# Linear attention and an RWKV channel mix: both head groups of batches 5 to 7 in one tiled block, and the last two tiles stored by one DMA a piece

## Chip, cores and metric

One core of one Trainium2 chip. The metric is the device time of one execution in microseconds (us); the median of three runs is given. A profile of one further execution shows where the time goes. PE is TensorE, DVE VectorE, ACT ScalarE, POOL GpSimd, SP SyncE.

## What is computed

q, k and v are [8 batches, 8 heads, 576, 64] in float32. Linear attention with two softmaxes gives x, which is read as [8, 576, 512] and goes through a channel mix with weights of 512 x 1024, 1024 x 512 and 512 x 512:

```python
q_s = softmax(q, axis=-1)                     # over head_dim
k_s = softmax(k, axis=2)                      # over the sequence
kv  = einsum('bhsd,bhse->bhde', k_s, v)       # 64 x 64 for each head
x   = einsum('bhsd,bhde->bhse', q_s, kv).transpose(0, 2, 1, 3).reshape(8, 576, 512)

x_prev = x shifted by one row (a zero row first)
xk = mu_k * x + (1 - mu_k) * x_prev
xr = mu_r * x + (1 - mu_r) * x_prev
k  = maximum(xk @ w_k, 0)
v  = k * k @ w_v
r  = sigmoid(xr @ w_r)
out = r * v                                   # float32, [8, 576, 512]
```

## The kernel before

**Stages.** A batch is worked in two head groups g = 0, 1 of four heads. For each group `attention(b, g)` loads q, k, v (three loads of 576 KB on POOL's queue, L213, into one of 11 "raw" buffers), takes the exponentials on ACT, sums and scales q on DVE, and casts v. On PE follow the small matrices KV = k_s' v (`kv`, L420: 36 matmuls of 64x64 tiles with 65 columns, the 65th being the sum that normalises k), on DVE the reciprocal of that sum (`rz`) and the weights (`w`), and on PE X = q_s kv (`x`, L577: eight matmuls of 64x64 tiles, four for the last 64 of the 576 columns and four for the first 512). X needs q turned; for batches 4 to 7 (`CROSS`) a DMA transpose that SP issues does that (`tq`). ACT copies X out of PSUM in two parts (`xb`, 512 columns from a pair of banks, and `xs`, the 64 spare columns), DVE shifts and mixes it into xk and xr.

The channel mix runs over units of up to 512 rows (`unit`: k matmuls L681, relu on ACT L660, square on DVE L670) and over 36 tiles of 128 rows (`tile_out`: r matmuls L714, tanh `th` on ACT L719, v matmuls L734, the gate `o` on DVE L740 that makes the output in a "th" buffer, stores `st` L750). The mix of batches 0 to 3 runs while the attention of later ones is made.

**Blocks on PE.** For batches 2 to 7 a PE block B(b, g) holds the X of the group before it ("pending") and the KV of its own group, so that X does not stand alone between full 128x128 matmuls. The spare 64 columns of X lie beside KV in one PSUM pair (columns 368 on, KV from 296), the 512 in the other pair. Only X of (2, 1) and of (7, 1), named in `ALONE`, have a block of their own. The last blocks of before are B50, B51, B60, B61, B70, B71 and X71.

**PSUM.** Four single banks mm_a to mm_d serve k, r and v; two pairs att_a and att_b serve the attention.

**Stores.** An output tile is 128 rows of a ring, two sequence positions j and j+1 of 64 rows each. `store` writes one half: 64 partitions of the buffer to 64 rows that lie 9 x 512 elements apart, as a destination of [64 rows][width]. Two such DMAs store a tile, both from SP's queue; in the last two tiles (34 and 35) the second goes by ACT's queue. Tile 35 is cut into two pieces of 256 columns, each with its own v matmuls, gate and two stores.

**The order.** What each engine does and in which order is not found at build time. `ORDER` is a list of the names of all operations in one line of time, with the buffer that each takes after the colon ("B51:1.0", "th35:1"), an engine ahead of "!" where there is a choice, and "^" for a load that is held until another operation is done ("load71q0^tq50"). `Plan.ordered` reads it and fails if an operation stands ahead of what it needs; semaphore waits follow from the data. "fill" and "fillgap" are matmuls on idle data in the start. A name with ".2" is the second operation of that name; "v35_0.2" is the first half of the v matmuls of tile 35's second piece.

Of the kernel before, what the change touches and what calls it, by code (L numbers as in the profile page):

```python
# [38 lines left out]
GAPS = 11  # L39
WHOLE = ((0, 0), (0, 1), (1, 0), (1, 1), (2, 0), (3, 0))  # L40
FUSED = (0, 1)
CROSS = (4, 5, 6, 7)
EARLY_UNITS = 3
ALONE = ((2, 1), (B - 1, 1))
# [5 lines left out]
ACT!load01k1:3 SP!load01k0 warm POOL!muload expq000:0 expq001 load00v^expq000 rsum000:0 rsum001  # L50
load01v expq010:1 wk00 expq011 rrec001 rrec000 rsum010:1 wide:0 wk01 expk000:0 rrec010 rsum011
wk10 mu:1 expk001 fillgap:2 fillgap.2:3 fillgap.3:2 fillgap.4:3 scale010:0 wk11 Z00:0 fillgap.5:2
fillgap.6:3 fillgap.7:2 fillgap.8:3 fillgap.9:2 fillgap.10:3 fillgap.11:2 rrec011 expk011:1
load11q0:4 scale011 widecopy rz00:0 scale001:1 T01:1 KV000 scale000 ACT!qt011:0 KV001 expk010
DVE!qt010 T00 rest mucopy kvn00:0 KV010 qt001:1 POOL!wp001:0 DVE!qt000 Z01 KV011 edge00 load10q0:5
wp000 X0010:3 rz01:1 load11q1 X0001:2 kvn01:1 edge01 x0010 wp010:1 load10q1 X0000:0 wp011 x0001a
X0100:1 load11v1:6 ACT!x0001b X0110:3 x0000a wr X0101:2 x0100b ACT!x0000b x0110 X0011:0 load11k1:7
DVE!x0101a x0100a k0_4:2 x0101b k1_7:3 x0011 k1_3:0 load10v1:8 k1_7.2 k1_3.2 relu1_7:0 k0_4.2
load11k0 k1_0:1 relu1_3:1 sq1_7 k0_5 expq110:2 k0_0:3 load11v0 k1_0.2 k0_0.2 relu0_4:2 rsum110:2
k1_4:0 relu1_0:0 k1_5:2 sq1_3 expq111 k1_2:1 sq0_4 k1_5.2 sq1_0 k1_2.2 rsum111 relu1_5:1 k1_4.2  # L60
cast111:0 k0_1 relu1_2:2 k0_6:2 sq1_5 wv0 relu1_4:0 k1_6:1 rrec110 expq101:1 sq1_2 k0_2:0
scale110:2 load10k1:9 k0_6.2 relu0_0:1 X0111:1 load10v0 rrec111 k0_7 expq100 rsum101:3 k1_6.2
k1_1:3 relu0_6:2 load10k0 k0_2.2 rrec101 k1_1.2 sq0_0 ACT!x0111 k0_3 rsum100 wv1 r0:2 relu1_1:1
sq0_6 expk111:2 wv2 r1:3 sq1_4 rrec100 th0:0 load20q0:10 scale100:0 relu1_6:2 r2:2 th1:1
load21q0:0 sq1_6 scale111 ACT!cast110 r3:1 sq1_1 relu0_2:0 scale101 T11:0 expk110 T10:1
ACT!cast101:1 KV11 qt101:2 load20v0:1 v3_0:3 qt110:1 sq0_2 th3:2 qt111 v0_0:0 rz11:2 expk101:0
cast100 kvn11:0 DVE!qt100 v1_0:1 edge11 expk100 wp110:0 edge10 DVE!wp111 X1100:0 KV10 x1100 v0_1
rz10:0 kvn10:1 X1111:0 POOL!wp100:1 X1101:1 x1111 v1_1 ACT!x1101 load31q0:2 X1001:0 th2:3 X1000:1
load20k0:3 ACT!x1001 v0_2 DVE!x1000 v3_1 load21v0:4 expq200:0 o0 v1_2 load21k0:5 k2_7:2 k2_3:0
rsum200:1 expq210:2 wp101 k2_7.2 v3_2 load30q0:6 relu2_7:2 o1 X1011:0 X1110:1 cast200:2 load30k0:7  # L70
rrec200 k2_3.2 o3 k2_1:2 load40q0:8 k2_0:1 relu2_3:1 x1011 k2_1.2 load30v0:9 expq310:1 sq2_3
k2_0.2 scale200:1 load41q0:10 k2_2:3 k2_6:0 relu2_1:0 load31k0:0 relu2_0:1 X1010:0 k2_2.2
expk200:1 sq2_0 k2_6.2 DVE!x1010 k2_5:2 load31v0:1 v2_0:1 relu2_2:1 sq2_1 rsum210:0 cast210:0
k2_4:3 load40k0:2 TKV20:0 relu2_6:0 sq2_2 rrec210 expk210:2 k2_4.2 rz20:1 sq2_6 k2_5.2 sq2_7
load40v0:3 v6_0:0 DVE!x1110 relu2_5:1 relu2_4:0 w20:0 v2_1 scale210:2 expq300:0 r5:2 load50q0:4
r6:3 qt20:0 rsum310:2 load50k0:5 v2_2 expk300:0 sq2_5 B21:1.0 sq2_4 o2 load41v0:6 th6:4 v6_1
rz21:2 xb20:0 w21:1 rsum300:3 r4:1 load50v0:7 xs20 qt21:1 r7:3 edge20 o6 th4:5 rrec300 X21:0.1
st6.2 diff20:0 th7:6 r8:0 th5:7 sc2001:0 scale300:0 v4_0:1 xb21:1 v5_0:3 xs21 sc2011:1 cast300:1
sc2010 v7_0:2 sc2000 edge21 rrec310 expq400:2 diff21:1 load70k0:9 TKV30:0 sc2100:2 expq410:0 v5_1
sc2101 load70v0:8 rz30:0 mix210 v4_1 cast310:2 load51v0:10 mix200 v7_1 o5 th8:8 v4_2 load51q0:1  # L80
sc2111:2 k3_1:3 st5.2 expk400:1 o4 w30:2 k3_3:0 st4 o7 relu3_1:2 load41k0:2 st0.2 expk310:2 sc2110
k3_7:1 mix201 st1 k3_0:3 sq3_1 st6 qt30:2 load51k0:0 scale310:1 st5 k3_2:2 relu3_0:1 st1.2
cast400:0 sq3_0 B31:1.0 rsum400:1 relu3_2:0 k3_6:3 load60k0:3 xs30:0 mix211 relu3_7:2 k3_5:2
relu3_3:1 rz31:1 sq3_2 xb30 w31:0 k3_4:1 sq3_3 sq3_7 relu3_6:0 r9:0 edge30 rrec400 diff30:0 qt31:0
# [12 lines left out]
sq5_2 v13_1 rz50:1 edge41 w50:0 mix400 expk600:2 r15:2 diff41:0 v15_1 expq610:0 o12 scale600:1
B51:1.0 th15:5 r14:0 expk700:0 sc4101:0 sc4100 r17:2 o15 mix410 st15.2 v17_0:3 th17:6 o13 th14:0
k6_0:2 tq51^load71k0:1 rz51:2 expq710:2 v17_1 w51:1 mix401 k6_1 o17 xs50:0 xb50 k6_4:1 sc4111:2
v16_0:0 st17 rsum610:3 expq700:1 st10 k6_6:3 st8.2 k6_5 edge50 relu6_0:0 sc4110 v16_1 st17.2  # L100
diff50:1 cast710:0 st12 k6_2:2 mix411 st13.2 relu6_4:2 B60:1.0 o16 st3.2 k6_3 xb51:1 rz60:0
sc5001:0 tq60^load71k0:2 k6_7 sc5000 sq6_0 r20:1 relu6_6:1 mix500 xs51 v14_0:0 relu6_2:0 sq6_6
w60:2 st13 sc5010:1 r18:3 sc5011 st16 edge51 th20:8 diff51:0 st9 r19:2 expk610:1 rrec610 st16.2
sc5101:2 v14_1 sc5100 st15 th19:6 sq6_2 mix510 v18_0:1 th18:2 sq6_4 cast610:1 o14 k7_7:2 sc5110:0
expk710:2 k7_0:3 scale610:0 B61:0.1 cast700:2 sc5111 tq61:0 v18_1 mix511 rsum700:0 xs60:1 k7_3:0
relu7_7:1 st12.2 relu7_0:0 st9.2 k7_4:2 relu7_3:2 xb60 r21:3 sq7_3 rz61:1 rsum710:2 k7_5:0
relu7_4:2 k7_2:2 edge60 w61:0 o18 B70:1.0 rrec700 sq7_4 mix501 v19_0:1 relu7_5:2 th21:1 diff60:1
r22:0 xs61:0 xb61 sq7_0 sq7_7 k7_1:3 scale700:2 relu7_2:0 v19_1 relu7_1:1 edge61 tq70:1 sq7_1
r26:2 rrec710 sq7_5 sq7_2 r23:3 th26:3 diff61:0 st14 v22_0:2 st10.2 th23:5 sc6110:2 rz70:2 sc6111
th22:7 k7_6:3 sc6100:0 o19 v20_0:0 scale710:1 relu7_6:1 r25:1 w70:1 tq71:2 sc6001:1 B71:0.1 sq7_6  # L110
th25:9 sc6101 v23_0:3 mix611 st14.2 sc6000 v21_0:1 mix610 rz71:0 v23_1 mix600 xs70:0 xb70 w71:2
v21_1 o23 v22_1 X71:0.1 o22 v20_1 sc6011:2 sc6010 k8_5:3 edge70 diff70:0 k8_3:2 o21 relu8_5:2
mix601 k8_0:3 relu8_3:0 sc7001:0 o20 k8_1:1 relu8_0:1 sq8_3 xb71:1 st20.2 k8_2:2 sq8_0 st18 k8_6:0
st20 relu8_2:0 relu8_1:1 st21 r28:3 st23 sq8_1 sc7000 r27:2 relu8_6:1 st18.2 mix700 xs71 th28:4
k8_4:1 edge71 sq8_5 diff71:1 r24:0 sq8_6 sq8_2 k8_7:3 th24:0 sc7100:1 sc7101 relu8_4:2 v27_0:0
sc7010:2 mix710 relu8_7:1 r29:1 sc7111:0 sq8_7 sq8_4 v24_0:3 th29:8 sc7110 th27:2 k9_4:1 k9_6:2
relu9_4:0 k9_3:1 v24_1 relu9_3:1 relu9_6:2 sq9_3 v26_0:1 o24 k9_1:2 sc7011 sq9_4 sq9_6 v25_0:3
relu9_1:1 v26_1 k9_2:2 o26 v25_1 relu9_2:0 v27_1 o25 k9_0:1 o27 mix711 k10_6:2 st27 st25 sq9_1
k9_7:3 relu10_6:2 st19 relu9_0:1 sq10_6 r30:0 st27.2 sq9_0 st26.2 mix701 k10_3:2 st24 k10_0:1
# [69 lines left out]
def graph(kn):  # L189
# [144 lines left out]
    def attention(b, g):  # L334
# [139 lines left out]
        else:  # L474
# [4 lines left out]
            def block():  # L479
                if turn_x:  # L480
                    turn_x[0](qtp)
# [144 lines left out]
    for b in range(B):  # L626
        for g in range(2):
            attention(b, g)
# [271 lines left out]
```

## Time and profile before

| | us |
|---|---|
| median of 3 runs (196.58 to 196.68) | 196.65 |
| the profiled execution | 196.49 |
| its span, first to last instruction | 194.7 |
| TensorE busy in it (95%) | 184.9 |
| DVE busy (76%) | 148.4 |
| ACT busy (69%) | 133.7 |
| POOL busy (24%) | 46.4 |

The granted TensorE clock is 0.995 of full over the span. In the rows of the timeline a line gives the start, the duration, the engine (PEld is the load of weights, SPq and ACTq the issuing of DMAs), the line of the code, the operation, output<-input, the shape and how many were grouped. The rows of waits give an engine and line, what it waited for, and the total, number and longest in us. In the windows each engine's busy time stands with the number of instructions, then the granted clock, the busy share of the 16 DMA engines and GB/s. In the DMA rows the last number is the median time from issue to landing.

### The profile page before, as it was taken

Reading aid. Unit: us, or ns where it says so; the run is one execution under the profiler, and the core shown is the slowest. Engines: PE = TensorE matmul, PEld = TensorE weight load, DVE = VectorE, ACT = ScalarE, POOL = GpSimd, SP = SyncE. Lnnn points to the kernel's source line nnn. Section 1 sums busy time; section 2 is a strip of 40 time slices with the busy share of each in tenths; the row PEclk is TensorE's granted clock in tenths of the full one; section 3 lists DMA queues with packets and bytes.
Section 4 is the critical chain, followed back from the end, with each engine's and each line's share of the span. In section 5 each row is a group of like instructions: output and inputs, shape, how many; then the busy total and the mean of one; then the engine's idle time right before and its main releaser. Section 6 shows DMA issues by size and latency. Waiting matters only on the chain.

```text
span 194.7 us, 4639 instructions
## 1 busy us (share of the span) xinstructions
PE 184.9 (95%) x1819; PEld 93.9 (48%) x1841; DVE 148.4 (76%) x343; ACT 133.7 (69%) x214; POOL 46.4 (24%) x76
## 2 busy tenths in 40 slices
PE   7897999999999999999999999999999999999990
PEld 2374755445545544465545644444444444444450
DVE  1886887689999999998998998999669247324431
ACT  3856999899999999489997988663175522621400
POOL 6857663885416303200700000000000000000000
PEclk9999999999999999999999999999999999999998
DMA  5999999999999999979997794144015003703855
GB/s 190 350 204 338 300 306 307 327 397 394 391 392 394 400 411 331 331 246 203 231 407 183 179 206 88 32 100 96 7 35 130 0 0 83 188 3 80 201 123 135
DMA packets 26069, 42.45 MB, mean 218 GB/s; under 512 B 11828, under 2 KB 15168, under 8 KB 26048
## 3 DMA queue, kind: packets, MB, share of 16 engines
q0 software_dynamic: 9504, 28.00, 43.8%
q1 hardware_dynamic: 15728, 12.72, 27.1%
q10 hardware_dynamic: 816, 1.44, 2.0%
q8 instruction: 14, 0.23, 0.5%
q14 instruction: 7, 0.06, 0.1%
HBM read 33.56 MB, written 9.44 MB: 221 GB/s over the span
## 4 chain that ended last, share of the span: by engine, by line
PE 80%; DVE 7%; DMA 6%; issue 2%; ACT 1%; POOL 1%; ACTq 0%; DVEq 0%; POOLq 0%
PE mm_c L681 10%; PE mm_b L734 9%; PE mm_a L734 8%; PE mm_d L734 8%; PE mm_b L681 8%; PE mm_d L681 7%; PE mm_c L714 5%; PE mm_c L734 4%; PE mm_a L681 4%; PE mm_d L714 4%; PE mm_a L714 3%; DMA mu_rows<-in_moe_mu_r_dram 3%; DMA raw_c<-in_q_dram 3%; PE mm_b L714 3%; DVE k L670 1%
## 5 line engine op out<-in xcount | busy, mean ns | idle before, releaser
L734 PEld LDWEIGHTS <-k 128*128 128x128 bf16 x296 | 28.1, 98 | 30.6 <-issue 0.7
L714 PEld LDWEIGHTS <-xr 128*128 128x128 bf16 x144 | 13.9, 98 | 16.4 <-issue 0.2
L670 DVE TENSOR_TENSOR k<-rel_b 128x512 bf16<-128x512 bf16 (+2 forms) x29 | 11.6, 399 | 8.9 <-ACT rel_b L660 8.8
L660 ACT ACTIVATE rel_a<-mm_c 128x512 bf16<-128x512 f32 (+1 forms) x11 | 6.6, 599 | 9.7 <-PE mm_c L681 9.6
L714 PE MATMUL mm_c<-wr,xr 128*128 128x512 bf16 x47 | 12.3, 379 | 0.1
L681 PEld LDWEIGHTS <-wk_aa 128*128 128x128 bf16 x88 | 8.4, 98 | 7.8 <-issue 0.2
L681 PEld LDWEIGHTS <-wk_ba 128*128 128x128 bf16 x88 | 8.3, 98 | 7.8 <-issue 0.4
L670 DVE TENSOR_TENSOR k<-rel_a 128x512 bf16<-128x512 bf16 (+2 forms) x24 | 9.6, 400 | 3.2 <-ACT rel_a L660 3.2
L670 DVE TENSOR_TENSOR k<-rel_c 128x512 bf16<-128x512 bf16 (+2 forms) x23 | 9.3, 403 | 3.4 <-ACT rel_c L660 3.3
L681 PEld LDWEIGHTS <-wk_ab 128*128 128x128 bf16 x88 | 8.4, 98 | 7.1 <-issue 0.5
L681 PEld LDWEIGHTS <-wk_bb 128*128 128x128 bf16 x88 | 8.5, 98 | 6.8
L734 PE MATMUL mm_b<-wv_a,k 128*128 128x512 bf16 x42 | 11.2, 379 | 0.1
L714 PE MATMUL mm_d<-wr,xr 128*128 128x512 bf16 x40 | 10.3, 379 | 0.0
L734 PE MATMUL mm_a<-wv_a,k 128*128 128x512 bf16 x38 | 10.2, 379 | 0.1
L734 PE MATMUL mm_d<-wv_a,k 128*128 128x512 bf16 (+1 forms) x38 | 9.8, 368 | 0.1
L681 PE MATMUL mm_c<-xk,wk_ba 128*128 128x512 bf16 (+3 forms) x34 | 8.6, 334 | 0.0
L681 PE MATMUL mm_c<-xk,wk_bb 128*128 128x512 bf16 (+3 forms) x34 | 8.6, 334 | 0.0
L714 PE MATMUL mm_a<-wr,xr 128*128 128x512 bf16 x31 | 8.2, 380 | 0.1
L660 ACT ACTIVATE rel_c<-mm_c 128x512 bf16<-128x512 f32 (+1 forms) x8 | 4.8, 595 | 4.5 <-PE mm_c L681 2.9
L681 PE MATMUL mm_c<-xk,wk_aa 128*128 128x512 bf16 (+2 forms) x28 | 7.4, 347 | 0.0
L681 PE MATMUL mm_c<-xk,wk_ab 128*128 128x512 bf16 (+2 forms) x26 | 7.0, 344 | 0.0
L660 ACT ACTIVATE rel_b<-mm_d 128x512 bf16<-128x512 f32 (+2 forms) x10 | 5.8, 577 | 1.5 <-PE mm_d L681 1.5
(352 smaller groups left out, 495.4 us busy)
## 6 DMA issues: line engine op xcount, KB each, us to landing
raw_k<-in_q_dram POOLq DMA_DIRECT2D x4, 576.0 KB, 8.1
raw_f<-in_k_dram POOLq DMA_DIRECT2D x3, 576.0 KB, 8.2
raw_a<-in_k_dram POOLq DMA_DIRECT2D x3, 576.0 KB, 11.5
out_dram<-th_b SPq DMA_DIRECT2D x10, 128.0 KB, 2.4
out_dram<-th_c SPq DMA_DIRECT2D x10, 128.0 KB, 2.4
raw_b<-in_v_dram POOLq DMA_DIRECT2D x2, 576.0 KB, 10.4
raw_d<-in_k_dram POOLq DMA_DIRECT2D x2, 576.0 KB, 8.8
raw_e<-in_v_dram POOLq DMA_DIRECT2D x2, 576.0 KB, 6.3
```

The costliest lines, as they stand in the source:

```text
L660: kn.nc.scalar.activation(out=kn.rels[rel.index][:, 0:width], in_=kn.bank(kf)[:, 0:width], func=ACT.Relu, scale=HALF_ROOT)
L670: kn.nc.vector.tensor_tensor(out=to, in0=src, in1=src, op=ALU.mult)
L681: kn.nc.tensor.matmul(kn.bank(kf)[:, lo:lo + n], lhsT=kn.wk[fc // 4][ct % 2][:, ct // 2, (fc % 4) * 128: (fc % 4) * 128 + 128], rhs=kn.xs[ ...
L714: kn.nc.tensor.matmul(kn.bank(rps), lhsT=kn.xs[1][:, ct, c:c + 128], rhs=kn.wr[:, ct, :], start=(ct == 0), stop=(ct == CT - 1))
L734: kn.nc.tensor.matmul(kn.bank(vps)[:, 0:width], lhsT=kn.k2[:, ft, at:at + 128], rhs=wv_of(ft)[:, part], start=(ft == 0), stop=(ft == FT - 1))
```

## The change

- **Joint blocks.** Batches 5, 6 and 7 (`JOINT`) have one block each, D5, D6, D7, in place of two. `joint_batch` puts the KV of both groups into one PSUM pair (columns 0 and 66 on) after the X of the groups that are pending, with their spare columns at 136 and 200 of the same pair. D5 holds X41 and KV50, KV51; D6 holds X50, X51, KV60, KV61; D7 likewise; XX7 holds X70 and X71. One reciprocal (`rz5`) and one weight operation (`w5`) serve both groups; the buffers `ws` and `rzs` are doubled for it. `attention` becomes a generator that stops at the block and goes on after it.
- **A pair of single banks.** The 512 columns of the X of group 1 that such a block takes (X41 too) go to a pair "pr" made of two of the single banks, mm_a and mm_b or mm_c and mm_d, and ACT copies them in two halves (`xb51a`, `xb51b`).
- **Stores.** For tiles 34 and 35 `store_both` writes a whole piece by one DMA: 128 partitions to a destination of [2][64 rows][width]. Tile 34 goes by SP, tile 35's columns 256 on by ACT and its first columns by SP.
- **Start.** 9 gap fills in place of 11, and the rows of mu lie in the last "th" buffer in place of one of their own.
- **Order.** `ORDER` is another text throughout. Among much else, the X matmuls of batch 1 stand otherwise among the v matmuls, the loads held by "^" change (six on POOL's queue from load61q0 on, behind tq41, the third of them load50v0; before, five from load71q0 on, behind tq50), and at the end v35_0 stands ahead of v35_1.2.

A set `TWO` of batches, and the code for it, is empty and has no effect.

```diff
-GAPS = 11
+GAPS = 9
+JOINT = (5,6,7)
+KVJ, XJ = 66, 136
-ALONE = ((2, 1), (B - 1, 1))
+ALONE = ((2, 1),)
+          ("pr", 0): [("mm", 0), ("mm", 1)], ("pr", 1): [("mm", 2), ("mm", 3)]}
...
-        pair = Slot("att")
+        late = b + 1 in JOINT or b == B - 1
+        pair = Slot("pr" if late and g else "att")
...
+            if pair.pool == "pr":
+                evs += [add("ACT", lambda u=u: copy_first(u), [made], [xb], [pair],
+                            name=f"xb{tag}{'ab'[u]}") for u in range(2)]
...
+    def two_turns(name, a, ready, given, kvs):
+        turns = list(pending)
+        pending.clear()
+        def block():
+            for g, turn in enumerate(turns):
+                turn[0](a, XJ + 64 * g)
+            for g, kv in enumerate(kvs):
+                kv(a, at=KVJ * g)
+        made = add("PE", block, ready + [d for t in turns for d in t[1]] + alone,
+                   [a] + [x for t in turns for x in t[2]],
+                   given + [x for t in turns for x in t[3]], name=name)
...
+    def joint_batch(b, parts):
+        a = Slot("att")
+        rz, w = parts[0][3:]
+        made = two_turns(f"D{b}", a, parts[0][1] + parts[1][1], parts[0][2] + parts[1][2],
+                         [p[0] for p in parts])
...
+    two_turns(f"XX{B - 1}", Slot("att"), [], [], [])
...
+            def store_both(queue, part=part, width=width):
+                jb = (RING * half + c) // 64
+                bb, j = jb // J, jb % J
+                dst = bass.AP(tensor=kn.out.tensor,
+                              offset=kn.out.offset + (bb * S + j) * C + part.start,
+                              ap=[[C, 2], [J * C, 64], [1, width]])
+                kn.queues[queue].dma_start(out=dst, in_=kn.ths[th.index][:, part])
...
-            for i in range(2):
-                queue = "ACT" if last and i else "SP"
-                add(queue, lambda i=i, q=queue, f=store: f(i, q), [o], [], [th],
-                    name=f"st{index}")
+            if last:
+                queue = "ACT" if len(parts) == 2 and part.start else "SP"
+                add(queue, lambda q=queue, f=store_both: f(q), [o], [], [th], name=f"st{index}")
+            else:
+                for i in range(2):
+                    add("SP", lambda i=i, f=store: f(i, "SP"), [o], [], [th], name=f"st{index}")
...
-    kn.ws = buffers("w", [128, 2, D], BF16)
+    kn.ws = buffers("w", [128, 2, 2, D], BF16)
-    kn.rzs = buffers("rz", [128, 2], F32)
+    kn.rzs = buffers("rz", [128, 2, 2], F32)
-    kn.mu_rows = const.tile([2, 2, 256], F32, name="mu_rows")
+    kn.mu_rows = kn.ths[-1][0:2, :].rearrange("p (m c) -> p m c", m=2)
```

The end of the order, before and after:

```diff
-... v35_0.2:3 st28.2 v33_0:2 o32 st32.2 v34_0:1 st32 v33_1 v34_1 o33 r35:0 st33 o34 v35_1.2
-st34.2 st34 v35_0:2 th35:1 st33.2 v35_1 o35.2 st35.4 st35.3 o35 st35.2 st35
+... v34_0:0 st28 v32_1 st31 st24.2 v35_0.2:3 o32 st28.2 v33_0:2 st32.2 r34:1 v33_1 th34:5 st32
+v34_1 o33 r35:1 st33.2 o34 st33 v35_0:2 th35:4 st34 v35_1.2 v35_1 o35.2 o35 st35.2 st35
```

More of the change, by code (lines that the diff above doesn't have):

```diff
@@ L55 @@
[L55 to L60, printed above, removed]
@@ new lines @@
+rrec000 expq010:1 rsum001 wk00 expq011 rsum010:1 wide:0 wk01 rsum011 expk001:0 wk10 rrec010 mu:1
+expk000 rrec011 fillgap:2 fillgap.2:3 fillgap.3:2 scale010:0 wk11 Z00:0 scale011 fillgap.4:2
+fillgap.5:3 fillgap.6:2 fillgap.7:3 expk011:1 load11q0:4 rrec001 T01:1 expk010 rz00:0 load11q1
+scale001:1 fillgap.8:2 fillgap.9:3 widecopy scale000 load10q1:5 KV001 qt010:0 KV000 rest ACT!qt011
+T00 Z01 kvn00:0 KV011 qt001:1 POOL!wp001:0 DVE!qt000 KV010 mucopy edge00 load10q0 wp000 X0010:3
+rz01:1 load11k1:6 X0000:0 kvn01:1 edge01 x0010 wp010:1 X0001:2 wp011 x0000a wr X0101:1 DVE!x0001a
@@ L127 @@
+sq10_7 v32_0:1 st25 th33:3 st27.2 v34_0:0 st28 v32_1 st31 st24.2 v35_0.2:3 o32 st28.2 v33_0:2
+st32.2 r34:1 v33_1 th34:5 st32 v34_1 o33 r35:1 st33.2 o34 st33 v35_0:2 th35:4 st34 v35_1.2 v35_1
+o35.2 o35 st35.2 st35
 """
@@ L339, in attention @@
             for n in ("eq", "ek", "vv", "stat", "qs", "qt", "rz"))
[L340 removed]
+        w = None if fused or (b in JOINT and g) else in_turn("w")
         c0 = S * (b % 4)
@@ L577, in x, with copy_first, copy_second @@
                         kn.nc.tensor.matmul(kn.half(slot, u)[two[r], to:to + n],
-                                            lhsT=kn.ws[w.index][two[u], r, :], rhs=by,
+                                            lhsT=kn.ws[w.index][two[u], wg, r, :],
+                                            rhs=by,
                                             start=True, stop=True)
-        def copy_first():
-            kn.nc.scalar.copy(out=kn.xbs[xb.index][:, :, 64:576], in_=kn.whole(pair))
-        def copy_second(other):
+        def copy_first(u=None):
+            to = kn.xbs[xb.index]
+            if u is None:
+                kn.nc.scalar.copy(out=to[:, :, 64:576], in_=kn.whole(pair))
+            else:
+                kn.nc.scalar.copy(out=to[:, u, 64:576], in_=kn.half(pair, u))
+        def copy_second(other, spare):
             kn.nc.scalar.copy(out=kn.xbs[xb.index][:, :, 576:640],
-                              in_=kn.whole(other)[:, :, XO:XO + 64])
+                              in_=kn.whole(other)[:, :, spare:spare + 64])
         def edge():
@@ L619, in attention, with block @@
             other = Slot("att")
-            alone.append(add("PE", lambda: x(other), [qcopy, wdone], [pair, other], [qt, w],
+            alone.append(add("PE", lambda: x(other, XO), [qcopy, wdone], [pair, other], [qt, w],
                              name=f"X{tag}"))
-            then(alone[-1], other)
+            then(alone[-1], other, XO)
         else:
             pending.append((x, [qcopy, wdone], [pair], [qt, w], then))
-    for b in range(B):
-        for g in range(2):
-            attention(b, g)
+    def two_turns(name, a, ready, given, kvs):
+        turns = list(pending)
+        pending.clear()
+        def block():
+            for g, turn in enumerate(turns):
[5 more added lines that the diff above has]
+                   given + [x for t in turns for x in t[3]], name=name)
+        for g in reversed(range(len(turns))):
+            turns[g][4](made, a, XJ + 64 * g)
+        return made
@@ new lines, in finish, with both @@
+    def finish(part, value):
+        try:
+            part.send(value)
+        except StopIteration:
+            pass
+    for b in range(B):
+        groups = [attention(b, g) for g in range(2)]
+        if b in JOINT:
+            done = joint_batch(b, [next(part) for part in groups])
+            for part in groups:
+                finish(part, done)
+        elif b in TWO:
+            parts = [next(part) for part in groups]
+            def both(parts=parts):
+                for slot, _, _, turn, kv in parts:
+                    turn(slot)
+                    kv(slot)
+            made = add("PE", both, parts[0][1] + parts[1][1] + alone, [p[0] for p in parts],
+                       parts[0][2] + parts[1][2], name=f"TT{b}")
+            for part in groups:
+                finish(part, made)
+        else:
+            for part in groups:
+                for _ in part:
+                    pass
```

222 lines of the change are left out of this document (121 added, 101 removed).

## The prediction

> **What bounds the kernel now.** I read the page's busy times first, then its chain, then the waits of TensorE, then the tail in order of time, and last the packets of the DMA queues.
>
> ```profile
> PE 184.9 (95%) x1819; PEld 93.9 (48%) x1841; DVE 148.4 (76%) x343; ACT 133.7 (69%) x214; POOL 46.4 (24%) x76
> ...
> PE 80%; DVE 7%; DMA 6%; issue 2%; ACT 1%; POOL 1%; ACTq 0%; DVEq 0%; POOLq 0%
> ```
>
> TensorE (PE) is busy for 184.9 of 194.7 us and holds 80% of the chain that ended last; DVE and ACT have a quarter of the span free. Where PE stands still is the next question. The first three rows are all its waits from 17.7 to 191 us, the next two the largest before.
>
> ```profile
> PE mm_d L734 <- issue: 0.2, 1, 0.2
> PE mm_b L734 <- issue: 0.2, 1, 0.2
> PE mm_a L734 <- DVE th_d L740: 0.2, 1, 0.2
> ...
> PE mm_a L303 <- DVE qt_c L250: 1.2, 1, 1.2
> PE mm_a L273 <- DMA mu_rows<-in_moe_mu_r_dram: 0.9, 1, 0.9
> ```
>
> Between 17.7 us and the last matmul PE waits 0.6 us in all. So every PE microsecond that the change saves there moves the end, and nothing that DVE, ACT or SP save there does. The end itself is a tail behind PE:
>
> ```profile
> 186.94 1.04 PE mm_b L734 x4
> ...
> 188.00 0.70 DVE th_d L740
> ...
> 188.72 0.55 ACTq L750
> ...
> 189.39 0.60 ACT th_b L719
> ...
> 190.02 0.42 DVE th_b L740
> ```
>
> The last matmuls of tile 34 end near 188.0, its gate op o34 runs to 188.70, ACT spends 0.55 us issuing tile 34's second store, and only then runs tile 35's tanh (189.39) that both gate ops of tile 35 need. The stores:
>
> ```profile
> 188.72 0.47 SPq L750 DMA_DIRECT2D out_dram<-th_d  x1
> 188.72 0.55 ACTq L750 DMA_DIRECT2D out_dram<-th_d  x1
> ...
> 190.36 0.41 DVE L740 SCALAR_TENSOR_TENSOR th_b<-th_b,mm_c 128x256 f32<-128x256 f32 x1
> 190.47 1.11 SPq L750 DMA_DIRECT2D out_dram<-th_b  x2
> 190.48 1.39 ACTq L750 DMA_DIRECT2D out_dram<-th_b  x2
> ```
>
> From 188.72 on, six DMAs of the last two tiles leave, three on each queue. The next rows are the packets of 191.5 to 193 us, with the two queues, and what a 64 KB store took from issue to landing.
>
> ```profile
> DMA packets 320, 0.26 MB, mean 175 GB/s; under 512 B 64, under 2 KB 320, under 8 KB 320
> ...
> q1 hardware_dynamic: 160, 0.13, 34.9%
> q10 hardware_dynamic: 160, 0.13, 33.3%
> ...
> out_dram<-th_b SPq DMA_DIRECT2D x1, 64.0 KB, 2.0
> out_dram<-th_b ACTq DMA_DIRECT2D x1, 64.0 KB, 2.3
> ```
>
> These are tile 35's four stores of 64 rows: 320 packets are 256 rows of 1 KB and 64 packets under 512 B. Sixty-four is 16 for each store: each closes with one small packet from each of 16 DMA engines, so a store whose outermost count is 64 runs on all 16, four rows to an engine.
>
> **The change part by part.** *Joint blocks.* A block of 64x64 tiles between full matmuls costs a change of mode twice. Two blocks of before give its price: pending X plus KV (batch 3), and X71 alone.
>
> ```profile
> 89.62 0.38 PE L681 MATMUL mm_c<-xk,wk_bb 128*128 128x256 bf16 x2
> 89.93 0.22 PE L577 MATMUL att_b<-qt_b,w_b 64*64 64x64 bf16 x4
> 89.98 0.39 PE L577 MATMUL att_a<-qt_b,w_b 64*64 64x512 bf16 x4
> 90.20 0.48 PE L420 MATMUL att_b<-vv_c,ek_c 64*64 64x65 bf16 x36
> 90.62 0.39 PE L681 MATMUL mm_a<-xk,wk_ba 128*128 128x512 bf16 x1
> ...
> 138.11 0.59 PE L734 MATMUL mm_c<-wv_c,k 128*128 128x512 bf16 x2
> 138.63 0.22 PE L577 MATMUL att_b<-qt_c,w_c 64*64 64x64 bf16 x4
> 138.69 0.39 PE L577 MATMUL att_a<-qt_c,w_c 64*64 64x512 bf16 x4
> 139.01 0.60 PE L734 MATMUL mm_a<-wv_b,k 128*128 128x512 bf16 x2
> ```
>
> A 512-column matmul follows the next after 0.216 us (four in 0.86 in the chain). From 138.11 to 139.01 are 0.90 us; two matmuls are 0.43, so X alone costs 0.47. Its four tiles run side by side, so its stream is 576 columns, 0.243; the rest, 0.225 us, is the change of mode. From 89.62 to 90.62 less two 256-column matmuls (0.22) is 0.78, so KV adds 0.31 and no second change. Batches 5 to 7 have seven blocks before (B50 to B71, X71) and four after (D5, D6, D7, XX7), with the same seven X and six KV: 3 x 0.225 = -0.67. In the new order the X matmuls of batch 1 fall into four tiled groups instead of three: +0.225. PE's sum: **-0.45 us**. Bounds: 0, if mode changes inside the longer blocks cost as much, and -0.67, if the early one hides.
>
> *Work beside it.* Six small reciprocal and six weight operations on DVE become three and three: cover is DVE's idle quarter, worth nothing on the path. A copy of X out of a PSUM pair takes ACT
>
> ```profile
> L582 ACT CAST xb_a<-att_a 128x1024 bf16<-128x1024 f32 x5 | 5.2, 1038 | 0.0
> L719 ACT ACTIVATE th_b<-mm_d 128x512 f32<-128x512 f32 x3 | 1.8, 596 | 1.9 <-PE mm_d L714 1.9
> ```
>
> 1.04 us, and as two halves of 512 about 2 x 0.6: +0.16 for each of four groups, under ACT's idle 31%. While it lasts two of the four single banks are held, and PE writes the other two; without that cover each block would cost PE up to 1.2 us (below). Fewer gap fills, the doubled small buffers and the rows of mu in a th buffer sit in the start, where PE waits for DVE and DMA: -0.1, between -0.4 and +0.2 (a third of its waits above, either way).
>
> *Order of tile 34 and 35.* With tile 34 stored by SP, ACT's 0.55 us of issue no longer stand ahead of th35. th35 then starts when r35 is done, and the last gate op waits for its matmuls alone: 0.15 us earlier than PE's gain makes it, and the last issue follows it at once, where before a second DMA came some 0.6 later on each queue. With stores as quick as now that is **-0.3 us** (0 if the last packets wait for tile 34's, -0.7 if both terms count in full).
>
> *The three wide stores.* Each new DMA takes 128 partitions, and its destination is written [2][64][width]: the outermost count is 2, where every store of before has 64. If an outer entry is what is dealt to a DMA engine, as four rows of 64 to each of 16 would have it, a store of 64 rows fills 16 engines and a new one only two, and both queues the same two. No row shows a store with an outer count below 64, so its price is bounded by the rate of one engine.
>
> ```profile
> 40.00:50.00 10.00, 9.89 (x114) 4.85 (x109) 9.48 (x19) 9.77 (x14) 6.15 (x10) 1.00 1.03 394
> ...
> 190.50:191.00 0.50, 0.00 (x0) 0.00 (x0) 0.28 (x1) 0.00 (x0) 0.00 (x0) 1.00 1.12 373
> 193.00:194.70 1.70, 0.00 (x0) 0.00 (x0) 0.00 (x0) 0.00 (x0) 0.00 (x0) 0.50 0.00 0
> ...
> DMA packets 464, 0.78 MB, mean 157 GB/s; under 512 B 82, under 2 KB 82, under 8 KB 464
> ...
> q1 hardware_dynamic: 464, 0.78, 67.7%
> ```
>
> The last two columns of the windows are the DMA engines' share and GB/s; the two rows at the end are of 177 to 182 us. Full engines move 394 GB/s, 24.6 each; the two tiles are 2 x 128 x 2 KB = 524,288 B, so two engines need at least 524,288 / 49.2 = 10.7 us. The stores of 177 to 182 give 0.78 MB in 67.7% of 80 engine-us, 14.4 GB/s each and 18.2 us; that is loose, since packet times overlap (the share passes 1 at 1.12). Those at 190.5 to 191 are nearest: 373 / (16 x 1.12) = 20.8 GB/s and 12.6 us; as a steady stream should lie nearer to full engines, I take **11.5**. Tile 34's store goes out at 188.72 - 0.45, so 188.3; the part of 2.0 us that is not transfer is about 1.8; the queue never runs dry after it. The last landing is 188.3 + 1.8 + 11.5 = 201.6. Before, no packet moves after 193.0, and the last store (the second of ACT's two, issued near 191.07, plus 2.3) lands near 193.3, 1.4 ahead of the span's end; so the new span is 203.0, **+8.3**. All savings on PE are in the 188.3.
>
> A rule bears on this. The Trainium skill, page "DMA: Bandwidth & Descriptors", section "Why a DMA increments its semaphore by 16 and not by 1", says that the number of engines is the largest one up to 16 that divides the outermost count above 1 of both patterns, and that the queues of SP and ACT take the lowest-numbered engines. By that, 128 and 2 give two engines and the sum just made; the 16 closing packets of the 64-row stores agree with it, and no run here shows a count of 2. The same page, section "Rules for kernel authors", speaks for the change instead: it advises one transfer of 128 partitions over two of disjoint halves. By that alone the sum would be the one without the +8.3.
>
> **The rivals.** *The stores spread over 16 engines* (the other side). Then tiles 34 and 35 are stored in half the DMAs, as fast as now. For it: 128 partitions stand outermost on the source, and the rows written are the same 2 KB and 1 KB. Against: the outer 2 of the destination. -0.45 - 0.3 - 0.1 = -0.85: 195.65 for the profiled run, **195.8** for the median. It decides where the transfer is dealt by rows.
>
> *Two engines for each queue, not the same ones.* SP then carries 384 of the 512 KB: 0.75 x 11.5 = 8.6, a landing at 198.7, a span of 200.1, +5.4: **202.1**. Nothing in the rows says which engines a narrow store takes; two queues that share all 16 now speak against it.
>
> *A wait moves into the joint blocks, with stores spread.* D5 needs the v of group 0 of batch 5, now the third of six loads held behind one DMA transpose. Loads so held in before:
>
> ```profile
> 92.61 0.71 POOL L213 DMA_DIRECT2D raw_g<-in_q_dram  x1 [12.55 <-ACT rel_b L660]
> ...
> 94.02 0.71 POOL L213 DMA_DIRECT2D raw_c<-in_v_dram  x1
> ...
> raw_c<-in_v_dram POOLq DMA_DIRECT2D x1, 576.0 KB, 7.2
> ```
>
> The third landed at 94.02 + 7.2 = 101.2, its cast is 1.2 us (1,024 columns take 1.04, it has 1,152), and D5 stands near 101.2 by a count of the matmuls ahead of it: PE would stop 1.2 us, and tile 17's v matmuls behind D5 with it. 195.8 + 1.2 = **197.0**. Against it: the new order issues these loads earlier. The held pair of banks would cost the same. That the joint blocks save nothing is the first rival with 196.3, within what can't be told.
>
> **How the numbers follow.** Two shared engines 0.76, the other pair 0.05, stores spread 0.13 (of which 0.02 with nothing saved), a wait in the joint blocks with stores spread 0.04, something else 0.02. The profiled 196.49 lies 0.16 under the median 196.65, so the likeliest is 196.49 + 8.3 + 0.16 = **205.0**; with 10.7 it is 204.2, with 18.2 it is 211.7. The range goes from 201.3 (the other pair with full engines, 0.75 x 10.7) to 209.0, about two thirds of the way from 204.2 to the loose bound, which leaves some 0.03 above and 0.17 below. A difference under 0.2%, 0.39 us, is about what a measurement of this kernel can't tell from none: faster 0.11 (stores spread and something saved), same 0.04 (nothing saved, and half of the waits), slower 0.85 (the rest).
>
> **What would show it.** After 190 us the DMA share near 2/16, 0.12, at some 49 GB/s, for ten microseconds with every engine idle; the three last stores landing 7 to 12 us after issue; each with 2 closing packets, not 16. PE should stop near 189.7 with seven tiled blocks turned into four of 0.47 + 0.31 and more, each costing one change of mode; th35 right behind r35. A DMA share above 0.5 in the tail, or a span under 196, proves the step on the stores wrong; PE waits of over 0.5 us at D5, D6 or XX7 prove wrong that their inputs are there; a last matmul later than 190.2 that the blocks save.

## The result

| | median us | runs |
|---|---|---|
| before | 196.67 | 196.58 to 197.43 |
| changed | 207.63 | 207.09 to 207.66 |

The ratio is 1.0542, with a 95% interval from 1.0511 to 1.0573: 11.0 us slower. Forecast were 205.0 in a range of 201.3 to 209.0. The profiled execution of the changed kernel took 207.63, its span is 205.9.

The page of the changed kernel, busy times:

```profile
PE 187.0 (91%) x1839; PEld 93.8 (46%) x1839; DVE 150.9 (73%) x342; ACT 133.8 (65%) x215; POOL 45.7 (22%) x74
```

PE's share of the span falls from 95% to 91% though its busy time rises: there is a stretch in which nothing computes. Its tail, in order of time, has the gate op of tile 34 (190.05), PE's last matmuls and the three wide stores (L846):

```profile
189.90 1.11 SPq L837 DMA_DIRECT2D out_dram<-th_d  x2
190.05 0.69 DVE L827 SCALAR_TENSOR_TENSOR th_f<-th_f,mm_a 128x512 f32<-128x512 f32 x1 [0.18 <-PE mm_a L821]
...
191.10 0.61 SPq L846 DMA_DIRECT2D out_dram<-th_f  x1
...
191.74 0.38 PE L821 MATMUL mm_c<-wv_c,k 128*128 128x256 bf16 x2
...
192.24 1.12 ACTq L846 DMA_DIRECT2D out_dram<-th_e  x1
192.65 0.53 SPq L846 DMA_DIRECT2D out_dram<-th_e  x1
```

The last issue ends near 193.2, and the span at 205.9. In the windows of the changed kernel, whose last two columns are the share of the 16 DMA engines and GB/s, that time looks so:

```profile
193.00:194.00 1.00, 0.00 (x0) 0.00 (x0) 0.00 (x0) 0.00 (x0) 0.00 (x0) 1.00 0.16 33
194.00:195.00 1.00, 0.00 (x0) 0.00 (x0) 0.00 (x0) 0.00 (x0) 0.00 (x0) 1.00 0.09 29
...
198.00:200.00 2.00, 0.00 (x0) 0.00 (x0) 0.00 (x0) 0.00 (x0) 0.00 (x0) 0.50 0.13 49
202.00:204.00 2.00, 0.00 (x0) 0.00 (x0) 0.00 (x0) 0.00 (x0) 0.00 (x0) 0.50 0.14 49
204.00:206.00 2.00, 0.00 (x0) 0.00 (x0) 0.00 (x0) 0.00 (x0) 0.00 (x0) 0.50 0.03 9
```

All compute engines stand at zero, and the share is 0.13, two sixteenths. The packets of 198 to 205.9 in it, and the queues:

```profile
DMA packets 280, 0.31 MB, mean 39 GB/s; under 512 B 6, under 2 KB 250, under 8 KB 280
...
q1 hardware_dynamic: 162, 0.19, 6.7%
q10 hardware_dynamic: 118, 0.12, 4.2%
```

Six small packets close three stores, two for each, where the 64-row stores of before closed with 16 each. Both queues move at once and together reach 49 GB/s; when SP's queue is alone at the end, from 203.6 to 204.2, it moves 48 by itself at the same share of 0.13. So they share the same two engines.

PE itself is later too. Its waits from 17.7 us on, in the changed kernel (the first belongs to the start):

```profile
PE mm_b L532 <- issue: 1.2, 1, 1.2
PE mm_b L593 <- ACT th_d L806: 0.9, 1, 0.9
```

The second is in block D5. Around it, in order of time, with two of POOL's six loads ahead:

```profile
91.44 0.72 POOL L216 DMA_DIRECT2D raw_j<-in_q_dram  x1 [10.72 <-ACT rel_a L747]
...
92.88 0.72 POOL L216 DMA_DIRECT2D raw_b<-in_v_dram  x1
...
101.79 0.59 PE L821 MATMUL mm_d<-wv_c,k 128*128 128x512 bf16 x2
...
101.98 1.15 ACT L356 CAST vv_c<-raw_b 128x1152 bf16<-128x1152 f32 x1 [2.09 <-DMA raw_b<-in_v_dram]
102.32 0.22 PE L593 MATMUL att_a<-qt_b,w_c 64*64 64x64 bf16 x4
102.37 0.38 PE L593 MATMUL mm_a<-qt_b,w_c 64*64 64x512 bf16 x1
...
103.04 0.59 ACT L806 ACTIVATE th_d<-mm_b 128x512 f32<-128x512 f32 x1
...
103.68 0.37 PE L593 MATMUL mm_b<-qt_b,w_c 64*64 64x512 bf16 x1 [0.93 <-ACT th_d L806]
...
104.65 0.60 PE L821 MATMUL mm_c<-wv_a,k 128*128 128x512 bf16 x2
```

The load of v of batch 5, issued third, lands 9.1 us later. ACT has waited 2.1 us for it with the cast, and the tanh of tile 14 stands behind the cast. The tanh frees mm_b, the second bank of the pair that X41 writes, so PE stops in the middle of D5.

### The profile page after: what moved, and what is told of

The parts are those of the page before. It is cut to its first block, busy times and chain, and to the rows that moved or that the text cites. A ratio compares the mean times of both kernels' runs of the same rounds, so it can differ in the third digit from the quotient of the medians.

```text
span 205.9 us, 4655 instructions
## 1 busy us (share of the span) xinstructions
PE 187.0 (91%) x1839; PEld 93.8 (46%) x1839; DVE 150.9 (73%) x342; ACT 133.8 (65%) x215; POOL 45.7 (22%) x74
## 4 chain that ended last, share of the span: by engine, by line
PE 74%; DMA 6%; DVE 6%; ACT 5%; issue 2%; POOL 0%; DVEq 0%; ACTq 0%
PE mm_c L821 8%; PE mm_c L768 8%; PE mm_a L821 7%; PE mm_d L768 7%; PE mm_b L768 7%; PE mm_a L768 6%; PE mm_d L821 6%; PE mm_b L821 5%; DMA raw_b<-in_v_dram 4%; PE mm_b L801 4%; PE mm_c L801 4%; PE mm_a L801 3%; PE mm_d L801 2%; DMA raw_a<-in_q_dram 2%; PE att_a L423 1%
## 5 line engine op out<-in xcount | busy, mean ns | idle before, releaser
L801 PE MATMUL mm_b<-wr,xr 128*128 128x512 bf16 x48 | 12.3, 379 | 0.0
L821 PE MATMUL mm_c<-wv_a,k 128*128 128x512 bf16 (+1 forms) x48 | 11.9, 370 | 0.0
L757 DVE TENSOR_TENSOR k<-rel_b 128x512 bf16<-128x512 bf16 (+2 forms) x24 | 9.5, 397 | 1.1 <-ACT rel_b L747 1.0
L747 ACT ACTIVATE rel_a<-mm_a 128x512 bf16<-128x512 f32 (+1 forms) x10 | 6.0, 598 | 3.9 <-PE mm_a L768 3.9
L747 ACT ACTIVATE rel_c<-mm_c 128x512 bf16<-128x512 f32 x6 | 3.6, 598 | 7.2 <-PE mm_c L768 7.2
L747 ACT ACTIVATE rel_a<-mm_c 128x512 bf16<-128x512 f32 (+2 forms) x8 | 4.6, 569 | 5.2 <-PE mm_c L768 5.1
L747 ACT ACTIVATE rel_c<-mm_b 128x320 bf16<-128x320 f32 (+2 forms) x8 | 4.2, 522 | 4.6 <-PE mm_b L768 4.6
L821 PE MATMUL mm_c<-wv_b,k 128*128 128x512 bf16 (+1 forms) x24 | 6.9, 371 | 0.0
L821 PE MATMUL mm_c<-wv_c,k 128*128 128x512 bf16 (+1 forms) x24 | 6.9, 371 | 0.0
L364 DVE TENSOR_REDUCE rsum_a<-eq_a 128x9 f32<-128x576 bf16 (+1 forms) x4 | 4.1, 1034 | 3.5 <-ACT eq_a L349 3.5
```

The costliest lines, as they stand in the source:

```text
L364: return kn.nc.vector.reduce_sum(out=sums(kn.rsums, u), in_=kn.eqs[eq.index][:, :, u, :], axis=AX.X)
L747: kn.nc.scalar.activation(out=kn.rels[rel.index][:, 0:width], in_=kn.bank(kf)[:, 0:width], func=ACT.Relu, scale=HALF_ROOT)
L757: kn.nc.vector.tensor_tensor(out=to, in0=src, in1=src, op=ALU.mult)
L801: kn.nc.tensor.matmul(kn.bank(rps), lhsT=kn.xs[1][:, ct, c:c + 128], rhs=kn.wr[:, ct, :], start=(ct == 0), stop=(ct == CT - 1))
L821: kn.nc.tensor.matmul(kn.bank(vps)[:, 0:width], lhsT=kn.k2[:, ft, at:at + 128], rhs=wv_of(ft)[:, part], start=(ft == 0), stop=(ft == FT - 1))
```

## The experiments

All times are medians beside runs of the kernel before on the same chip. The first four went together (before: 196.79).

**Two stores a piece.** The changed kernel, each wide store cut in two on its own queue:

```diff
-            def store_both(queue, part=part, width=width):
-                ...
-                              ap=[[C, 2], [J * C, 64], [1, width]])
-                kn.queues[queue].dma_start(out=dst, in_=kn.ths[th.index][:, part])
+            def store_both(queue, f=store):
+                for i in range(2):
+                    f(i, queue)
```

> The changed kernel with each wide store cut into two of 64 rows on the same queue; all else as changed. Theory (narrow stores run on two DMA engines, and apart from them the new order ends TensorE some 1.8 us later than before): TensorE's last matmul near 192 us, the second store of each queue near 193, last landing 195.2, span about 196.7, median about 198.5, so some 9 us faster than the changed kernel and 1.8 slower than before. Rival 1 (TensorE's delay explains most of the 11 us, the stores little): 205 or more. Rival 2 (the blocks and the order save what was forecast, the delay being of the one execution): 195.8.

198.45 (197.81 to 198.72), ratio 1.0072 [1.0051, 1.0093]. The wide stores cost 207.63 - 198.45 = 9.2 us, and all else that changed costs 1.7 by the medians, 1.4 by the ratio (the six runs lie in two groups, near 197.9 and 198.5). Both rivals fall.

**The wide stores alone, on the kernel before.** `store_both` and its calls are put into the kernel before, and its order's end names one store for each piece:

```diff
-... v35_1.2 st34.2 st34 v35_0:2 th35:1 st33.2 v35_1 o35.2 st35.4 st35.3 o35 st35.2 st35
+... v35_1.2 st34 v35_0:2 th35:1 st33.2 v35_1 o35.2 st35.2 o35 st35
```

> The kernel before with the last two tiles stored by one DMA a piece, tile 34 and tile 35's first columns by SP, the others by ACT; nothing else changed. Theory (two engines, both queues on the same): 524,288 B at the 49 GB/s seen after 196 us in the changed kernel take 10.7 us from a first packet near 188.7 + 1.8; landing 201.2, span 202.7, median about 204.6, DMA share 0.13 for 10 us. Rival (another pair of engines for each queue): 202. Rival (the narrow stores cost only together with the new order): within 1 us of before.

206.33 (206.02 to 206.92), ratio 1.0481 [1.0451, 1.0511]: the same cost without the new order, so the rivals fall, but 1.7 us over the figure. Two rows of this kernel:

```profile
194.00:196.00 2.00, 0.00 (x0) 0.00 (x0) 0.00 (x0) 0.00 (x0) 0.00 (x0) 0.76 0.13 45
...
out_dram<-th_a SPq DMA_DIRECT2D x2, 128.0 KB, 5.9
```

The rate is under 49 GB/s at first, as in the changed kernel (33 and 29 GB/s in the two windows above), and the two stores of tile 33 take 5.9 us in the median, not 2.4: the second of them is issued behind tile 34's and lands after 9.6, so its shares on the two engines wait there. These are two things that the figure left out; how much each costs was not taken apart.

**Only tile 34 wide.** The changed kernel with tile 35's pieces stored as two of 64 rows:

```diff
-                add(queue, lambda q=queue, f=store_both: f(q), [o], [], [th], name=f"st{index}")
+                add(queue, lambda q=queue, f=store_both if len(parts) == 1 else store_two: f(q), ...)
```

> The changed kernel with only tile 34 (256 KB) stored by one DMA; tile 35's pieces by two of 64 rows on the same queue. Theory (two engines, time in proportion to the bytes): 5.4 us of transfer from 191.1 + 1.8, landing 198.3, span 199.8, median about 201.5. Rival (a fixed cost of each wide store): two thirds of the cost gone, near 201.4 only if the cost of all three is 9 us and equal, so the packets tell: with the theory two engines are busy to 198.3 and the others are idle from 196; with a fixed cost no engine is busy.

204.18 (204.06 to 204.23), 2.7 over the figure. Half of the bytes cost 204.18 - 198.45 = 5.7 of 9.2 us. Tile 35's stores run on all engines, but two sixteenths of them queue behind tile 34's rows: those of 64 KB land after 6.0 us (ACT) and 7.6 (SP), where before they took 2.3 and 2.0. The landing stands last:

```profile
196.00:198.00 2.00, 0.00 (x0) 0.00 (x0) 0.00 (x0) 0.00 (x0) 0.00 (x0) 0.51 0.52 133
198.00:200.00 2.00, 0.00 (x0) 0.00 (x0) 0.00 (x0) 0.00 (x0) 0.00 (x0) 0.50 0.12 46
...
out_dram<-th_e SPq DMA_DIRECT2D x2, 64.0 KB, 7.6
```

From 198 to 200 two engines work on, so it is no fixed cost with idle engines. What I left out were that queueing and the slow first microseconds.

**62 rows, and 48.** Is it the third level of the pattern, the 128 partitions, or the count? The kernel before, each 64-row store of tiles 34 and 35 cut in two plain lists of rows on the same queue (CUT is 62, or 48):

```diff
+                for lo, hi in ((0, CUT), (CUT, 64)) if last else ((0, 64),):
...
-                              ap=[[J * C, 64], [1, width]])
+                                  ap=[[J * C, hi - lo], [1, width]])
```

> The kernel before with each 64-row store of tiles 34 and 35 cut into one of 62 rows and one of 2, same queue, each a plain [rows][width]. Theory (a store runs on as many engines, up to 16, as divide its outermost count: 62 gives two, 2 gives two): the same 524,288 B on two engines, DMA share 0.13 for 10 us, median 205 to 207. Rival (a destination of three levels, or 128 partitions in one DMA, is what was slow; a plain list of rows is dealt to all engines): 197.5 to 198, the price of six more issues. Rival (the rows are dealt one by one, 62 to 16 engines as four and three): the same 197.5 to 198.

> As the run with 62 and 2 rows, with 48 and 16 rows instead. Theory and rivals alike (16 divides both counts): all 16 engines, and the price of six more issues, two more on each queue behind the last gate at 0.55 us each: 197.5 to 198. If it is slow too, the number of DMAs and not the count of rows is the cause.

With 62 and 2 rows 205.60 (205.51 to 206.38), ratio 1.0432 [1.0373, 1.0492]; with 48 and 16 rows 196.89, ratio 1.0006 [0.9975, 1.0037]; before 196.72. The first row is the packets of 194 to 203.9 with 62 rows, the second is a window there, the third the landing of a 48-row store:

```profile
DMA packets 339, 0.37 MB, mean 38 GB/s; under 512 B 28, under 2 KB 284, under 8 KB 339
...
198.00:200.00 2.00, 0.00 (x0) 0.00 (x0) 0.00 (x0) 0.00 (x0) 0.00 (x0) 0.50 0.14 48
...
out_dram<-th_b SPq DMA_DIRECT2D x1, 48.0 KB, 1.7
```

62 plain rows fare as the pattern with 2 outermost: 48 GB/s, 0.14 of the engines. 62 = 2 x 31 has 2 as its largest divisor up to 16; 48 and 16 are multiples of 16. So it is the outermost count, not the levels, the 128 partitions or the number of DMAs; six more issues cost 0.2 us, which the interval does not tell from nothing, and not the 0.8 to 1.3 expected. All of it agrees with the rule of the Trainium skill, page "DMA: Bandwidth & Descriptors", section "Why a DMA increments its semaphore by 16 and not by 1", for the counts 2, 62 and 48. No count whose largest divisor up to 16 lies between 2 and 16, such as 60, was run, so the runs do not exclude a cruder rule: two engines for whatever is no multiple of 16.

**v of batch 5 loaded first.** On the run with two stores a piece:

```diff
-... w40:1 load61q0^tq41:9 sq4_7 ... cast510:0 r16:0 load50v0:1 xs40:0
+... w40:1 load50v0^tq41:1 load61q0:9 sq4_7 ... cast510:0 r16:0 xs40:0
```

> As the run with two stores a piece, and the load of v of batch 5 group 0 issued first of the six loads held behind the transpose of group 1 of batch 4, not third. Theory (this load, by the cast that waits for it on ACT and the tanh of tile 14 behind that cast, holds a bank that block D5 needs): D5 no longer waits, 1.3 us less than the run with two stores a piece, about 197.2. Rival (D5 waits for ACT's own backlog): the same as the run with two stores, 198.5. Rival (another of the six loads is late next): between the two or slower.

196.81 (196.72 to 197.38), ratio 1.0004 [0.9989, 1.0018]: 1.6 us less than with the load third (1.3 by the ratios), where the theory said 1.3. D5 in this kernel runs through:

```profile
101.51 0.59 PE L821 MATMUL mm_d<-wv_c,k 128*128 128x512 bf16 x2
102.03 0.22 PE L593 MATMUL att_a<-qt_b,w_c 64*64 64x64 bf16 x4
...
102.60 0.51 PE L423 MATMUL att_a<-vv_a,ek_b 64*64 64x65 bf16 x36
103.04 0.82 PE L821 MATMUL mm_c<-wv_a,k 128*128 128x512 bf16 x3
```

**The tanh ahead of the cast.** The run with two stores a piece, load third, "th14:3 cast500:2" in place of "cast500:2 ... th14:3". This went with the next two (before: 196.69).

> The changed kernel with two stores a piece (load of batch 5's v third, as changed), and on ACT the tanh of tile 14 ahead of the cast of that v. Theory (D5 waited for the bank that the tanh frees, because the tanh stood behind a cast that waited for the load): X41 goes at once and only KV50 waits for the cast, which lands 1.1 us after the load at 102: D5's block falls from 2.4 to 1.5 to 2.0 us, median 197.6 to 198.1. Rival (D5 waits for the load itself, whatever stands on ACT): 198.45, no change. Rival (the tanh was late for another reason): no change.

197.37 (197.18 to 198.16), ratio 1.0039 [1.0023, 1.0054]: 1.1 us less (0.7 by the ratios), though the load is as late (issued at 92.99, it lands after 8.9 us). The rivals fall; the median is 0.2 under the range that the theory gave. PE's only wait in this kernel from 100 to 106 us, and the matmuls on both sides of D5:

```profile
PE att_a L423 <- ACT vv_c L356: 0.5, 1, 0.5
...
101.86 0.59 PE L821 MATMUL mm_d<-wv_c,k 128*128 128x512 bf16 x2
...
104.04 1.04 PE L821 MATMUL mm_c<-wv_a,k 128*128 128x512 bf16 x4
```

Less the two matmuls (0.43), D5 takes 104.65 - 101.79 - 0.43 = 2.43 us in the changed kernel, 104.04 - 101.86 - 0.43 = 1.75 here, and 103.04 - 101.51 - 0.43 = 1.10 with the load first. So about half of what D5 lost, 0.68, was a bank held by a tanh that stood behind a waiting cast, and the other half, 0.65, the late v itself.

**Batch 1 as before, and the tail on both queues.** With the load first, two stores a piece, the X groups of batch 1 set as before the change; and then, in addition, tile 35's pieces with one store on each of SP and ACT.

```diff
-X1100:0 expk101:0 DVE!wp111 v0_0:2 qt101 expk100 cast100 DVE!x1100 ... KV10 sq1_6 X1111:0 ... v3_1
+v0_0:2 expk101:0 DVE!wp111 X1100:0 qt101 expk100 cast100 KV10 DVE!x1100 ... sq1_6 ... v3_1 X1111:0
-... X1001:0 ACT!x1101 v0_1 load30q0:7 ACT!x1001 X1000:1
+... v0_1 X1001:0 ACT!x1101 load30q0:7 X1000:1 ACT!x1001
```

and in the second of the two:

```diff
-                    f(i, queue)
+                    f(i, queue if len(parts) == 1 else ("SP", "ACT")[i])
```

> The run with two stores a piece and v of batch 5 loaded first, and the X matmuls of batch 1 grouped as before the change (X1100 with KV10, X1111 with X1101, X1001 with X1000). Theory (the new order of batch 1 costs one change of mode and two waits of TensorE, 0.7 us, which eats what the joint blocks save): the tiled groups between 32 and 39 us fall from 4.1 to 3.4 us, median about 196.1, faster than before by 0.6. Rival (the waits are for DVE's work and only move to the next group): 196.8, as now.

> As the run with batch 1 regrouped, and tile 35's pieces stored by one DMA of 64 rows on each of SP and ACT instead of two on one. Theory (the last issue on SP is then some 0.3 us earlier, and the end follows it): about 195.8. Rival (the last packets are limited by the DMA engines, not by the issue): 196.1, as without.

196.91 (ratio 1.0015 [0.9999, 1.0030]) and 197.06 (1.0018 [1.0005, 1.0031]): neither gains, as the rivals had it (their figures were 196.8 and 196.1). In the first of them PE has a new wait at the v matmul that was moved ahead:

```profile
PE mm_c L821 <- ACT rel_b L747: 0.8, 1, 0.8
```

**The start of before with joint blocks.** All operations up to the v matmuls of batch 1 in the order of before (11 gap fills), from there the new order with the load first, two stores a piece; banks and th buffers are renamed where the two meet. A second kernel puts each last store on both queues. Before: 196.51.

```diff
-... wp101 ... load21k0:5 ... load30q0:7 ...
+... load21v0:4 load21k0:5 load30q0:7 expq200:0 load30v0:6 wp101 o0 X1011:0 X1110:1 ...
```

> Joint blocks with the order of before up to the v matmuls of batch 1, then the new order (banks and th buffers renamed to fit), v of batch 5 loaded first, two stores of 64 rows a piece. Theory (the new order loses 0.7 us of TensorE around batch 1 and the joint blocks save 0.6; each stands alone): tiled groups of batch 1 near 3.4 us as before, last matmul near 189.6, median about 196.2, 0.5 under before. Rival (TensorE's gain is lost again behind batch 1, since DVE and ACT set the pace there): 196.8.

> As the run with the start of before, each of the last stores as one DMA of 64 rows on SP and one on ACT, tile 34's behind the tanh of tile 35 on ACT. Theory (SP's six issues behind the gate of tile 33 set the last landing): about 0.3 us less than that run, 195.9. Rival (the end follows the last gate and its own two issues): no difference.

200.61 (198.76 to 201.97) and 201.37 (201.01 to 202.41): both miss. Where the halves meet, POOL makes the weights of X1011 (wp101) behind a row of loads, three of which come after load21v0, and issuing each load keeps POOL busy for 0.7 us. From the first of the two kernels come the wait of PE, the last of those loads with the weights behind it, and the clock (the third number from the end):

```profile
PE att_a L531 <- POOL wp_b L520: 2.8, 1, 2.8
...
39.60 0.71 POOL L215 DMA_DIRECT2D raw_g<-in_v_dram  x1
40.33 0.87 POOL L520 TENSOR_TENSOR wp_b<-kvn_b,mu_wide 128x128 bf16<-128x128 f32 x2
...
38.00:41.20 3.20, 0.33 (x5) 0.11 (x4) 1.86 (x2) 1.60 (x2) 3.18 (x7) 1.00 0.94 338
41.20:44.60 3.40, 3.34 (x19) 1.35 (x20) 0.69 (x1) 0.00 (x0) 2.79 (x5) 0.53 0.96 347
```

Last, the same with wp101 ahead of those loads (before: 196.72):

```diff
-load21v0:4 load21k0:5 load30q0:7 expq200:0 load30v0:6 wp101 o0
+load21v0:4 wp101 load21k0:5 load30q0:7 expq200:0 load30v0:6 o0
```

> As the run with the start of before, and the mixed weights of batch 1 (wp101) on POOL ahead of the three loads behind which they stood there. Theory (those loads waited on POOL for free buffers, wp101 behind them, TensorE 2.8 us for wp101, and its clock was then granted at half for 3 us): all 4.2 us come back, last matmul near 189.7, median 196.1, 0.5 under before. Rival (POOL is late there anyhow): between 196.8 and 199.

197.07 (196.75 to 198.0), ratio 1.0024 [1.0009, 1.0039]. 3.5 us come back, not the 4.2 expected, and PE still waits for the same weights:

```profile
PE att_a L531 <- POOL wp_b L520: 0.7, 1, 0.7
```

Between 196.8 and 199, as the rival had it. The loads had not waited for buffers, as I had supposed: POOL issued them back to back, and three times 0.7 is the 2.1 us by which the wait fell. No version measured here is faster than the kernel before; the nearest, the load first with two stores a piece, is equal to it.

## Why the prediction was right

**The stores.** The step that decided held in each part: two engines, both queues the same two, 11.5 us of transfer taken (the windows show the wide stores' packets from about 193 to past 204). Its price was 205.0 - 195.8 = 9.2 us against the same kernel with stores spread, and 9.2 is what the run with two stores a piece shows. That it agrees to a tenth is luck: the 11.5 was chosen between 10.7 and 12.6, and on the kernel before the same stores cost 206.33 - 196.79 = 9.5. The upper bound, 18.2, was as loose as called; the lower, 10.7, misses only the first three microseconds at some 30 GB/s. That an outermost count of 2 leads to two engines was an inference when it was made; the runs with 62 and 48 rows show that the outermost count decides in plain lists too. The first rival, the stores spread over 16 engines as in the advice that the prediction names for the change, would have given 195.8 and falls by the 9.2. (Two slips in the sums change nothing here: 0.75 x 10.7 gives 201.5 as the lower end and not 201.3, and the -0.1 for the start stands in the 195.8 but not in the 205.0.)

**The joint blocks.** Sized rightly. XX7 and D6 of the changed kernel, each with the matmuls around it:

```profile
114.41 0.81 PE L801 MATMUL mm_c<-wr,xr 128*128 128x512 bf16 x3
115.15 0.22 PE L593 MATMUL att_b<-qt_a,w_a 64*64 64x64 bf16 x4
...
116.39 0.82 PE L821 MATMUL mm_d<-wv_a,k 128*128 128x512 bf16 x3
...
142.37 0.59 PE L821 MATMUL mm_c<-wv_c,k 128*128 128x512 bf16 x2
...
143.51 0.60 PE L768 MATMUL mm_d<-xk,wk_aa 128*128 128x512 bf16 x2
```

XX7 is 143.51 - 142.37 - 0.43 = 0.71, D6 is 1.98 - 0.65 = 1.33; one change of mode of 0.225, 0.243 for each X and 0.31 for each KV give 0.71 and 1.33. (The example of a block that the prediction puts into batch 3 is B41, of batch 4; its cost is the same.) D5 without its wait is 1.10, where the same prices give 1.09. So the three changes of mode, 0.67, are saved.

**What failed makes the 2.6 us between 205.0 and 207.63.** The forecast took 0.85 us off the kernel for blocks, start and tail, and the run with two stores a piece is 1.7 slower than before instead. The term of the sum that was mis-sized is PE's, -0.45: PE's last row of matmuls starts at 191.74 and not 189.3 (189.76 before). Tile 34's store, from which the sum counts, so goes out at 191.10 and not 188.3. Two of the prediction's own signs of being wrong are there: a wait of PE over 0.5 us at D5, and a last matmul later than 190.2. Three pieces are seen.

- *D5's wait.* It is the third rival, "a wait moves into the joint blocks", to which 0.04 was given, and which came together with the narrow stores, not instead of them. Its price was put at 1.2 us; D5 takes 2.43 us in the changed kernel instead of 1.10, 1.33 more, and 1.6 us of the median (1.3 by the ratios) come back when the load goes first. I had the load and its cast (landing put at 101.2, measured 101.96) and held against it that the order issues the loads earlier; the third goes at 92.88 and not 94.02, but takes 9.1 us to land and not 7.2. I had not followed what stands behind the cast on ACT.
- *Batch 1.* I counted one change of mode more, 0.225. The first of the new groups, X1100 in the changed kernel, with the largest wait behind it:

```profile
31.92 1.03 PE L821 MATMUL mm_a<-wv_a,k 128*128 128x512 bf16 x4
32.98 0.76 PE L532 MATMUL att_a<-qt_c,wp_a 64*64 64x288 bf16 x8
33.73 1.02 PE L821 MATMUL mm_c<-wv_a,k 128*128 128x512 bf16 x4
...
PEld L532 <- DVE wp_a L521: 0.5, 1, 0.5
```

It costs 33.73 - 31.92 - 0.86 = 0.95 us, where X alone costs 0.47: PE waits 0.5 us for weights that DVE makes. Read in the same way, the tiled groups from 32 to 45 us take 4.6 us instead of 3.7, of the 0.9 more 0.225 for the change of mode that was counted. (Between these groups the trace of before lacks the record of one full matmul: two weight loads stand beside one matmul at 34.19, and two are taken off.)

```profile
34.18 0.11 PEld L734 LDWEIGHTS <-k 128*128 128x128 bf16 x2
34.19 0.39 PE L734 MATMUL mm_a<-wv_b,k 128*128 128x512 bf16 x1
```

In three other orders the waiting moved (to v0_0, to X1011) and did not go. What sets the pace there was not isolated and stays open; so does whether the joint blocks would bring their 0.67 us with a start that fits them.
- *SP's queue.* Tile 34's gate op ends at 190.74, but its store goes out at 191.10, behind the two issues of tile 33 (189.90 and on). I had put it right behind the gate op.

The PE part adds up: 0.33 from the start (the first k matmul at 18.03 against 17.70), 0.9 from batch 1 and 1.33 from D5, less 0.67 for the blocks, are 1.9 of the 1.98 us by which the last row is later than before. SP's queue adds its 0.36 behind that.

The tail gave what was said, about: from PE's last row of matmuls to the end of the span are 194.7 - 189.76 = 4.94 us before and 195.0 - 190.21 = 4.79 with the load first and two stores a piece, 0.15 of the 0.3. The start varies by as much as its term: the first k matmul began between 17.60 and 18.09 in profiled executions of the changed kernel and its variants that share its start.

## What to carry to other kernels

Look at the outermost count of both patterns of every DMA that the end waits for: 64 rows ran on 16 DMA engines, 2 x 64 and 62 on two. Fewer DMAs are no gain when the merged pattern leads with a small number; here three DMAs in place of six cost 9.2 us. And when a block of PE is given a bank, follow what stands ahead of its release on the releasing engine: a cast that waits for a load delays a tanh that has all it needs.

## What was not expected of the hardware

A wait of PE of 2.8 us was followed by 3.4 us at a granted clock of 0.53 (windows of the run with the start of before): when a later order cut the wait to 0.7, 3.5 us came back for 2.1 of waiting. By an estimate from these rows the low clock is worth 3.4 x 0.47 = 1.6 us, and with the 2.1 that is about the 3.5. Two engines alone first moved 29 to 33 GB/s for some three microseconds and then 49; no run here shows why. The second queue is not the reason: from 196 to 197 us SP's queue still moves alone in the changed kernel, at 53 GB/s.
